# Performer attention and Fourier mixing on one core: head pairs on 128 partitions, alternating PE halves, rows turned through DRAM, 512-row channel blocks, a listed PE order

## The chip, the cores and the metric

The kernel runs on one core of one Trainium2 chip. The metric is the device time of one execution in microseconds; a median over several executions is given. A ratio "to before" is the mean time of one kernel's fast runs over the mean of the old kernel's fast runs of the same rounds on the same chip, so it is not quite the ratio of the medians.

Engine names are those of the profile: PE multiplies matrices, PEld is its weight load, DVE, ACT and POOL are the elementwise engines, SP issues transfers.

Two figures of mine recur. *Work* is the number of PE instructions of each kind, each at the spacing of starts that it has when nothing is waited for at full clock. *Lost* time is a stretch of the trace less the work whose starts fall in it. It covers both waiting and half-clock running.

## The reference, cut to what matters

```python
# q, k, v: (8, 8, 576, 64) float32; omega: (128, 64)
def phi(x):                                   # random features, 128 of them
    h = einsum('bhsd,md->bhsm', x, omega) - sum(x*x)/2
    return exp(h - max(h)) / sqrt(128)
q_p, k_p = phi(q*scale), phi(k*scale)
kv  = einsum('bhsm,bhsd->bhmd', k_p, v);  z = sum(k_p, axis=2)
att = einsum('bhsm,bhmd->bhsd', q_p, kv) / (q_p . z + 1e-6)
x   = att as (8, 576, 512)
u   = x + real(fft(fft(x, axis=1), axis=2))   # row and channel Fourier mix
un  = (u - mean(u)) / sqrt(var(u) + 1e-6)     # over the 512 channels
out = u + relu(un @ w_ch1) @ w_ch2            # 512 -> 2048 -> 512, weights float64
```

## The kernel before

Attention takes each head's 576 rows as 6 groups of 96 partitions (97 for the queries, whose rows are already put in the order that the folded Fourier transform wants). All six matmuls of one head's half of the array come one after the other:

```python
for i in range(2):                            # the two heads of a pair
    rows = slice(D * i, D * i + D)            # 64 of the 128 array rows
    kp = big_tile("kp")
    for r in range(R):                        # R = 6
        nc.tensor.matmul(kp[0:PR, ...], lhsT=kT[rows, r, :], rhs=omT[rows, :])
    kes.append(features(kp, PR, "ke"))
    # ... the same for qp, then kvp and ndp per head
```

Attention's result stays in SBUF, the mix works on it there, and the channel part takes the two halves of a batch, 289 rows each, as the moving operand; its second product comes out transposed and is turned back:

```python
for fc in range(NFC):                         # 16
    for dc in range(NDC):                     # 4
        nc.tensor.matmul(hp[:, 0:NK], lhsT=w1[...], rhs=un_t[:, dc, :], ...)   # NK = 289
    # ReLU to ht, on DVE for odd fc, on ACT for even
for dc in range(NDC):
    for fc in range(NFC):
        nc.tensor.matmul(op_[:, 0:NK], lhsT=w2[...], rhs=hs[fc][:], ...)
    # copy to SBUF, 128x128 transposes (otp), add, store
```

The float64 weights are narrowed to float32 on the chip, in 64 pieces of 256 columns, each with seven DVE instructions and one POOL addition. [cut: loads, tables, mix]

## Time and profile before

| | before |
|---|---|
| median | 1755.1 us (1749.4 to 1755.7) |
| PE busy | 1648 us, 94% of the span |
| PE work at full rate | 1523 us |
| lost before 400 us | 155 us |
| lost after 400 us | 71 us |

PE is busy all the time, but a busy PE is not a PE at its full rate. The prediction works from single starts; its 1528 us of work is the same sum from rounder prices.

### The profile page before, as it was taken

To read this page: it belongs to the slowest core of one execution; us is meant where nothing else is said; L and a number is where in the kernel's file an instruction comes from. 1 tells how busy PE (TensorE), PEld (TensorE's weight loads), DVE (VectorE), ACT (ScalarE), POOL (GpSimd) and SP (SyncE) were. 2 spreads that over 40 slices of the span, in tenths; PEclk is the share of its full clock that TensorE was granted. 3 is DMA by queue.
4 is the path that set the end of the run, shared out by engine and by line. 5 is a ranking of instruction groups with operands and counts; after the bars stand their busy time and mean duration, and the time that the engine had idled before them with its cause. 6 is when DMAs were issued, how large, how long until landed. Compare 5 with 4: busy or idle time off the path is not lost.

```text
span 1748.5 us, 21376 instructions
## 1 busy us (share of the span) xinstructions
PE 1648.2 (94%) x8897; PEld 1341.4 (77%) x8897; DVE 664.4 (38%) x1554; ACT 343.7 (20%) x609; POOL 233.2 (13%) x327
## 2 busy tenths in 40 slices
PE   6976888999999999999999999999999999998998
PEld 6864666877888788886888778887888778886776
DVE  5778776324233332414333332324233242333010
ACT  2211112112222221312122121212122121211000
POOL 2237332021000300021000300012000210012000
PEclk9995887999999999999999999999999999999999
DMA  6332222001010001101011010101011010000000
GB/s 136 80 81 68 72 87 77 21 8 27 22 41 21 16 19 28 41 8 28 21 35 27 1 35 21 48 8 28 21 30 26 7 28 22 20 1 14 0 14 14
DMA packets 125012, 56.92 MB, mean 33 GB/s; under 512 B 115762, under 2 KB 116018, under 8 KB 124916
## 3 DMA queue, kind: packets, MB, share of 16 engines
q1 hardware_dynamic: 119248, 37.83, 9.2%
q0 software_dynamic: 5120, 16.78, 3.1%
q8 instruction: 71, 1.16, 0.3%
q10 hardware_dynamic: 548, 0.94, 0.2%
q14 instruction: 25, 0.20, 0.0%
HBM read 46.09 MB, written 9.44 MB: 32 GB/s over the span
## 4 chain that ended last, share of the span: by engine, by line
PE 82%; DVE 8%; POOL 4%; DMA 3%; issue 1%; ACT 1%; POOLq 0%; DVEq 0%; ACTq 0%
PE hp L451 27%; PE op L470 25%; PE kvp L278 5%; PE qp L263 5%; PE kp L254 5%; PE ndp L304 4%; DMA raw<-in_moe_w_ch_dram 3%; PE yp L352 3%; PE eps L289 2%; DVE st L403 2%; POOL x L399 2%; PE tps L203 1%; PE otp L486 1%; PE fp L436 1%; PE tp L422 1%
## 5 line engine op out<-in xcount | busy, mean ns | idle before, releaser
L470 PE MATMUL op<-ht,w 128*128 128x289 f32 x2048 | 530.4, 413 | 7.1 <-POOL w L179 7.1
L451 PE MATMUL hp<-unT,w 128*128 128x289 f32 x2048 | 528.0, 411 | 1.8 <-DVE ht L460 1.7
L470 PEld LDWEIGHTS op<-ht,w 128*128 128x128 f32 x2048 | 384.6, 192 | 113.2 <-POOL w L179 8.2
L451 PEld LDWEIGHTS hp<-unT,w 128*128 128x128 f32 x2048 | 382.7, 191 | 113.7 <-issue 6.4
L460 DVE TENSOR_SCALAR ht<-hp 128x289 f32<-128x289 f32 x128 | 58.8, 459 | 372.2 <-PE hp L451 372.2
L122 POOL MEMSET v<- 96x12 f32 x32 | 3.8, 118 | 867.1 <-PE kvp L278 858.9
L254 PEld LDWEIGHTS kp<-omT,kT 64*96 64x96 f32 x768 | 98.4, 180 | 24.4 <-issue 16.6
L254 PE MATMUL kp<-omT,kT 64*96 64x128 f32 x768 | 113.9, 301 | 2.9 <-DVE qT L247 1.6
L263 PE MATMUL qp<-omT,qT 64*97 64x128 f32 x768 | 109.8, 296 | 6.9 <-DVE rstd L406 4.0
L462 ACT ACTIVATE ht<-hp 128x289 f32<-128x289 f32 x128 | 52.9, 413 | 291.6 <-PE hp L451 291.6
L278 PEld LDWEIGHTS kvp<-v,ke 96*128 96x128 f32 x768 | 103.4, 209 | 6.8 <-issue 1.1
L263 PEld LDWEIGHTS qp<-omT,qT 64*97 64x97 f32 x768 | 100.2, 181 | 10.8 <-ACT qT L241 5.1
L278 PE MATMUL kvp<-v,ke 96*128 96x65 f32 x768 | 105.3, 291 | 0.0
L221 ACT ACTIVATE ke<-ke 96x768 f32<-96x768 f32 x64 | 53.9, 842 | 215.3 <-DVE ke L215 215.3
L389 DVE SCALAR_TENSOR_TENSOR bmp<-ab,bmp 97x65 f32<-97x65 f32 x96 | 25.7, 328 | 175.2 <-ACT bmp L385 175.2
L304 PEld LDWEIGHTS ndp<-kv,qeT 128*97 128x97 f32 x768 | 82.2, 180 | 9.5 <-ACT qeT L295 1.6
L213 DVE TENSOR_REDUCE kemx<-kp 96x6 f32<-96x768 f32 x64 | 60.8, 950 | 71.4 <-PE kp L254 71.4
L492 DVE TENSOR_TENSOR x<-x,otp 97x512 f32<-97x512 f32 x48 | 32.3, 679 | 138.4 <-PE otp L486 138.4
L304 PE MATMUL ndp<-kv,qeT 128*97 128x65 f32 x768 | 82.7, 262 | 0.5 <-DVE kv L286 0.4
L480 ACT ACTIVATE ot<-op 128x289 f32<-128x289 f32 x64 | 26.5, 413 | 283.1 <-PE op L470 283.1
L295 ACT ACTIVATE qeT<-eps 128x582 f32<-128x582 f32 x64 | 42.0, 657 | 195.7 <-PE eps L289 180.6
L179 POOL TENSOR_TENSOR w<-ta,rest 128x256 f32<-128x256 f32 x64 | 53.8, 840 | 171.1 <-DVE rest L176 171.1
(73 smaller groups left out, 1413.5 us busy)
## 6 DMA issues: line engine op xcount, KB each, us to landing
raw<-in_moe_w_ch_dram POOLq DMA_DIRECT2D x64, 256.0 KB, 3.1
kn<-in_k_dram SPq DMA_DIRECT2D x64, 144.0 KB
qn<-in_q_dram SPq DMA_DIRECT2D x64, 144.0 KB
v<-in_v_dram SPq DMA_DIRECT2D x64, 144.0 KB
out_dram<-x SPq DMA_DIRECT2D x40, 192.0 KB
out_dram<-x SPq DMA_DIRECT2D x8, 190.0 KB
cs_sb<-k_cs ACTq DMA_DIRECT2D x1, 325.1 KB
sn_sb<-k_sn ACTq DMA_DIRECT2D x1, 325.1 KB
```

The lines of the kernel that those rows point to most:

```text
L179: nc.gpsimd.tensor_tensor(out=dst, in0=ta[:].bitcast(F32), in1=rest[:], op=ALU.add)
L213: nc.vector.tensor_reduce(mx[:], pr4, axis=AX.X, op=ALU.max)
L221: nc.scalar.activation(out=e[:], in_=e[:], func=AF.Exp, scale=SCALE)
L254: nc.tensor.matmul(kp[0:PR, r // 3, r % 3 * MF : r % 3 * MF + MF], lhsT=kT[rows, r, :], rhs=omT[rows, :],)
L263: nc.tensor.matmul(qp[0:CP, r // 3, r % 3 * MF : r % 3 * MF + MF], lhsT=qT[rows, t0 : t0 + CP], rhs=omT[rows, :],)
L278: nc.tensor.matmul(kvp[:, 0 : D + 1], lhsT=kes[i][:, r, :], rhs=v1[:, i, r, :], start=(r == 0), stop=(r == R - 1),)
L304: nc.tensor.matmul(nd[:, r, :], lhsT=qeT[:, r, :], rhs=kv[:])
L352: nc.tensor.matmul(yp[:, 0:NK], lhsT=fold[:, c, n, :], rhs=tab[:, c, :], start=(c == 0), stop=(c == NC3 - 1),)
L451: nc.tensor.matmul(hp[:, 0:NK], lhsT=w1[:, dc, 128 * fc : 128 * fc + 128], rhs=un_t[:, dc, :], start=(dc == 0), stop=(dc == NDC - 1),)
L460: nc.vector.tensor_scalar(ht[:], hp[:, 0:NK], 0.0, None, op0=ALU.max)
L462: nc.scalar.activation(out=ht[:], in_=hp[:, 0:NK], func=AF.Relu)
L470: nc.tensor.matmul(op_[:, 0:NK], lhsT=w2[:, fc, 128 * dc : 128 * dc + 128], rhs=hs[fc][:], start=(fc == 0), stop=(fc == NFC - 1),)
```

## The change

Its intent: PE does less, and the start overlaps better. Two heads of a pair share 128 partitions; their matmuls alternate between the upper and lower half of the array (or the left and right), so that two can run side by side. Attention's rows go to DRAM in plain order; the mix (the Fourier part) fetches the second half of the rows turned (in reversed order) by a gather, a transfer by a list of row numbers; the *fold* then adds and subtracts the two halves, first into the tile `half`, before the Fourier products `yp`; the mix's result goes through DRAM again, and the channel part takes blocks of 512 rows regardless of batches. The second product makes rows directly. PE's instructions follow a list that a small generator scheduler writes; other engines are ordered as before.

The core of the diff:

```diff
-            for i in range(2):
-                rows = slice(D * i, D * i + D)
-                kp = big_tile("kp")
-                for r in range(R):
-                    nc.tensor.matmul(kp[...], lhsT=kT[rows, r, :], rhs=omT[rows, :])
+            for j in range(3):
+                for par in range(2):
+                    rows = slice(D * par, D * par + D)
+                    nc.tensor.matmul(ps[:, par, MF * j : MF * j + MF],
+                        lhsT=kqT[rows, 3 * t + j, :], rhs=omT[rows, :])
 [cut: kvp alternates row halves, ndp column halves in the same way]
+        for c in range(NC3):
+            nc.gpsimd.indirect_dma_start(
+                out=x[:, NC3 + c, :], out_offset=None, in_=rows[:, :],      # 97 partitions
+                in_offset=bass.IndirectOffsetOnAxis(ap=turned[:, c : c + 1], axis=0))
+        yield 0.0, 5.0
 [cut: fold; first half of the sum on DVE, the difference on POOL, as before]
-                    nc.tensor.matmul(hp[:, 0:NK], lhsT=w1[...], rhs=un_t[:, dc, :], ...)
+                    nc.tensor.matmul(hp[:], lhsT=w1[...], rhs=unT[:, dc, :], ...)   # 512 rows
-                    nc.tensor.matmul(op_[:, 0:NK], lhsT=w2[...], rhs=hs[fc][:], ...)
+                    nc.tensor.matmul(yp[:], lhsT=hs[fc][:, 128*i : 128*i+128], rhs=w2[:, fc, :], ...)
-        ta = cvt.tile([128, n], U32, name="ta", tag="ta")
+        ta = cvt.tile([128, n], U32, name="ta", tag="ta", bufs=1)      # also tb and rest
+    with tc.manual_schedule(engines={mybir.EngineType.PE}):
+        streams = [weights(), mixing(), pairs(0), pairs(1), channels()]
 [cut: each stream's "yield work, latency" is the list's estimate in us; the first stream
  that is ready goes next]
```

## The prediction

> **What bounds the kernel now.** I read the page first (busy shares and the chain of work that ended last), then the table by stretches of time, then the timeline, because a busy PE is not yet a PE at its peak.
>
> ```profile
> PE 1648.2 (94%) x8897; PEld 1341.4 (77%) x8897; DVE 664.4 (38%) x1554; ACT 343.7 (20%) x609; POOL 233.2 (13%) x327
> ...
> PE 82%; DVE 8%; POOL 4%; DMA 3%; issue 1%; ACT 1%; POOLq 0%; DVEq 0%; ACTq 0%
> ```
>
> PE is busy for 94% of the span and carries 82% of the chain. So the kernel is bound by TensorE; other engines matter where they make it wait. Where that is, the table by stretches tells (columns: stretch, length, then busy time of PE, weight loads, DVE, ACT and POOL, granted clock, DMA share, GB/s):
>
> ```profile
> 0.00:127.00 127.00, 98.73 (x481) 92.17 (x481) 86.98 (x242) 27.41 (x37) 35.05 (x60) 1.00 0.42 100
> 127.00:185.00 58.00, 38.35 (x133) 28.07 (x134) 50.99 (x133) 9.65 (x19) 38.06 (x46) 0.59 0.23 65
> 185.00:312.00 127.00, 112.35 (x558) 88.14 (x557) 84.75 (x250) 22.65 (x37) 36.12 (x58) 0.87 0.26 77
> ...
> 312.00:1612.00 1300.00, 1268.20 (x7192) 1032.46 (x7191) 430.41 (x909) 273.29 (x491) 123.92 (x164) 1.00 0.09 23
> 1612.00:1748.00 136.00, 130.54 (x538) 100.58 (x537) 11.31 (x22) 10.72 (x26) 0.00 (x0) 0.98 0.03 9
> ```
>
> Until 312 us PE issues 1172 matmuls, against 7192 in the next 1300 us: 3.8 per us and then 5.5. In the start DVE works 223 of 312 us, mostly on narrowing the weights, and PE waits for it. What a matmul costs when nothing is waited for is in the timeline (start, length, engine, line, shapes, count), from one group's start to the next group's:
>
> ```profile
> 12.08 2.87 PE L254 MATMUL kp<-omT,kT 64*96 64x128 f32 x12
> ...
> 643.39 1.16 PE L304 MATMUL ndp<-kv,qeT 128*97 128x65 f32 x12
> 644.39 1.50 PE L278 MATMUL kvp<-v,ke 96*128 96x65 f32 x12
> 645.73 0.67 PE L289 MATMUL eps<-ident,qe 97*128 97x97 f32 x6
> 646.24 4.10 PE L451 MATMUL hp<-unT,w 128*128 128x289 f32 x16
> ...
> 664.06 1.55 PE L254 MATMUL kp<-omT,kT 64*96 64x128 f32 x12
> 665.45 1.47 PE L263 MATMUL qp<-omT,qT 64*97 64x128 f32 x12
> 666.85 4.16 PE L470 MATMUL op<-ht,w 128*128 128x289 f32 x16
> ```
>
> Per instruction: ndp 1.00/12 = 83 ns, kvp 1.34/12 = 112, eps 0.51/6 = 85, features (kp, qp) 2.79/24 = 116, against busy means of 262 to 301 ns in the table by lines, which count the pipeline's depth too. In the chain of waits the last 128 op matmuls take 31.15 us, 243.4 ns each: 289 columns at 1.2 per ns are 240.8, plus 2.6. A written f32 matmul is two instructions (384 kp matmuls in the code, 768 in the trace); a transpose is one.
>
> Priced so, PE's work in the old kernel is: channel mixing 4096 x 243.4 ns = 997 us. Attention per head pair: features 48 x 116, kvp 24 x 112, ndp 24 x 83, 24 transposes x 84 = 5.57 + 2.69 + 1.99 + 2.02 = 12.3 us, for 32 pairs 393. Fourier part 192 yp x 243 + 192 ab x 109 + 144 ab x 86 ns = 80. Transposes for the normalised rows 192 x 84 ns = 16, of the output 192 x 109 ns = 21, the flips (fp) 48 x 0.43 us = 21. In all 1528 us, so about 220 us of the span is not work at full rate. Counted with the same prices, about 158 us of the work falls before 311 us, so 153 of the 220 are lost in the start, the other 67 to waits later.
>
> **What the Trainium skill says.** (1) "TensorE: Matmul & The Clock Gate", Part 1: a PE with idle gaps is held at half its clock. The trace agrees: twelve kp take 2.87 us at 12.08 and 1.55 at 664.06. The clock column's 1.00 for the first stretch is then only a stretch without a record. (2) The same page, Part 3 (packing small matmuls): with 64 rows or columns in use, instructions on other row or column groups run side by side[...]. No group in this trace alternates its half, so the trace can't confirm it; the change rests on this. (3) "TensorEngine Tiling (Array Packing)", Key Properties: changing the tiling mode drains the array. The trace has something like it: single starts show 334 ns from an hp to a kp that follows, in place of 243, and 199 from a qp to an hp in place of 109, so 0.09 us a switch. (4) "DMA: Bandwidth & Descriptors", Specifications: transfers under 512 B do not reach line rate. The old kernel's loads are already so (115,762 of 125,012 packets), with DMA engines 9% busy later on; the new row stores in 256 B pieces should be borne likewise.
>
> **The change part by part.**
> Channel mixing in nine blocks of 512 rows instead of sixteen of 289: 9 x 128 = 1152 written matmuls, 2304 instructions. By the slope above, 512/1.2 + 2.6 = 429 ns; the new list's own 3.45 us for eight is 431. 2304 x 431 ns = 993 us: saves only 4. The pad rows were few and the fixed part is small.
> The second product now writes rows, not columns: the 192 output transposes go (-21). Rows are turned by an indirect transfer: the flips go (-21).
> Row transposes for the norm: 36 tiles x 4 = 144 of 128 columns, x 109 ns = 16: no change. Fourier part: same matmuls, 80.
> Attention per pair: 18 transposes of 128 x 109 ns = 2.0 us; 36 feature instructions, 36 kvp, 36 ndp. Without overlap of the halves: 36 x 109 + 36 x 112 + 36 x 56 (64 columns and 65 moving, 65/1.2 + 2.6) = 9.9, total 11.9 against 12.3: the fuller partitions alone buy next to nothing, since time goes by columns and the counts hardly fall. With overlap the features and kvp halve: 2.0 + 2.3 (the list's own figure for kvp), ndp 1.4 (list), total 7.7 us. Over 32 pairs 246 us, -147. Against it more mode switches: four stretches a pair (two of features, kvp, ndp), eight switches x 0.09 x 32 = 23 us.
> Work: 993 + 246 + 80 + 16 = 1335, with the switches 1358 us.
>
> **The start.** The chain is attention of batch 0, stores and reads through DRAM, mix, stores, reads, norm, first block. The order of w1 by output columns lets the first block start before all of it is there. But DVE is loaded: each narrow is 2.6 us of DVE (166 us over 64), each pair 6 x 0.95 + 0.3 + 0.5 + 0.9 = 7.4. With twelve pairs (88), two mixes (18), a norm and evictions (14) that is some 285 us by the point where the last w2 piece is there, and ta, tb and rest have one buffer now, so a narrow also waits for POOL's 0.84 us of the narrow before. I put the dense part's begin at about 310 us, with about 190 us of work done: 120 us lost, against 153.
> **Later waits.** Two pair streams take steps one after the other and share two large PSUM buffers. A feature tile is freed only after reduce and subtract (1.9 us), so the second stream's feature step waits about 3 us for the first's: 14 x 3 = 42. Last division to first yp: 1.3 us of DVE, two DRAM trips of estimated 2.5 and 5, fold 4.1, that is 13 to 16 us where the list allows 11; about 3 us a batch, 21 in seven. After that, a long stretch of nothing but blocks and row transposes, dense. The end: one addition and one store, 6 us.
> Sum: 1358 + 120 + 42 + 21 + 6 = 1547. The list was made to fill such waits with 3.45 us pieces of channel work, and some of what I add singly falls together, so I take 20 off: 1527 us.
>
> **Rivals.**
> A: the halves do not run side by side (the f32 passes, or the shared PSUM, serialise them). Then attention costs 11.9 us a pair and the time is 1527 + 32 x 4.2 = 1660. For it: nothing in this trace shows overlap. Against it: the code separates the halves into banks or partitions, and its stated 2.3 us for 36 kvp (64 ns) and 1.4 us for 36 ndp (39 ns) are below any serial price.
> B: the fixed PE order turns latencies into stalls: DRAM round trips, the fold on POOL (3.45 + 1.81 + 2 x 1.0 us), PSUM waits. If each batch loses 15 us more, and each pair 1.5, it is 1527 + 105 + 42 = 1674. For it: a late arrival holds all later PE work. Against it: after the list's PACE gaps only about half the kernel holds attention; the rest is channel work with no such wait.
> C: the start is much better than I think, channel work from 200 us on with w2 arriving in time: 60 us lost, 1467. For it: the old kernel started its channel work at 185 us already. Against it: its DVE was the limit then, and the amount of narrowing is unchanged.
> D: the reordered rows make DMA the bound. Estimated bytes grow from 57 to about 105 MB, 70 GB/s over the span; the first stretch already moves 100. I give it little.
>
> **Range and chances.** C below and A or half of B above give 1430 to 1620 us for 8 in 10. Even A with the waits as they are stays over 2% below 1755. Slower would take A and B together. Predicted 1527 us; faster 0.95, within 2% 0.03, slower 0.02.
>
> **What would show it.** Features, kvp and ndp of the new kernel: starts 55 to 64 ns apart in alternating groups (39 for ndp) if the overlap is real, 109 to 112 if A holds. Channel matmuls 429 to 433 ns apart. The first channel matmul at 150 to 200 us, and dense PE from about 310. Idle of PE before feature groups by DVE if the PSUM waits are real; before yp by DVE or DMA for B. PE's total falling by some 170 us of work, with losses of about 190 us beside it: if the work falls so and the time does not, the list made the waits and my sizes of them are wrong.

## The result, and the profile after

The changed kernel takes 1614.5 us (median of 4 runs, 1613.9 to 1616.3), the old one 1752.6 in its runs so far; the ratio is 0.921 (0.919 to 0.924). That is 8% faster. It lies inside the predicted range of 1430 to 1620, by 6 us, and 87 us above the predicted 1527.

The page's busy shares and the chain that ended last, of the changed kernel:

```profile
PE 1430.2 (89%) x7009; PEld 810.2 (50%) x7009; DVE 562.8 (35%) x1269; ACT 243.2 (15%) x389; POOL 304.3 (19%) x387
...
PE 68%; DMA 10%; DVE 7%; POOL 5%; issue 4%; ACT 0%; SPq 0%; POOLq 0%; DVEq 0%; ACTq 0%
```

PE has 218 us less to do by busy time, but its share of the chain fell from 82 to 68% and transfers came up from 3 to 10%. The kernel became shorter and waits more. The timeline of the changed kernel in a stretch at full clock (start, length, engine, line, shapes, count):

```profile
612.58 1.61 PE L272 MATMUL pp<-omT,kqT 64*128 64x128 f32 x24
614.12 3.70 PE L537 MATMUL op<-w,ht 128*128 128x512 f32 x8
...
619.22 0.94 PE L272 MATMUL pp<-omT,kqT 64*128 64x128 f32 x12
620.08 3.70 PE L537 MATMUL op<-w,ht 128*128 128x512 f32 x8
623.62 1.63 PE L394 MATMUL yp<-sn_sb,fold 97*128 97x289 f32 x6
625.18 2.23 PE L299 MATMUL kvp<-v,e 64*128 64x65 f32 x36
627.34 0.68 PE L409 MATMUL ab<-cd_sb,y 128*97 128x129 f32 x4
```

From one group's start to the next: features 1.54/24 = 64 ns and 0.86/12 = 72, kvp 2.16/36 = 60; ndp, at 601.87 in the same view, takes 1.20/36 = 33. In the old kernel these were 116, 107 to 112 and 83. Single starts within such a group lie about 7 ns apart and then a long gap: the two halves start nearly together. The prices include the switches at a group's ends. The slope of the prediction holds too: 243.4 ns for 289 columns and 109 for 128 (prediction) are 1.2 columns per ns, which gave 429 for 512, and 429 was measured. So the pieces of PE's work come out thus:

| | predicted | measured |
|---|---|---|
| channel matmuls, 2304 | 993 us (431 ns) | 989 us (429 ns) |
| attention, 32 pairs, with switches | 246 + 23 | 247 |
| Fourier part, row transposes | 96 | 95 |
| **work** | **1358** | **1331** |
| lost in the start (measured: before 400 us) | 120 | 200 |
| later waits (42 + 21, less 20) | 43 | 77 |
| end | 6 | 4 |
| **span** | **1527** | **1612** |

The work fell by 192 us. The waits did not shrink by 57 us as predicted; they grew by 55, from 226 to 281. The question for the experiments is where. The table by stretches, of the kernel before and then of the changed one (columns as in the prediction):

```profile
400.00:1200.00 800.00, 783.79 (x4464) 638.82 (x4463) 265.92 (x560) 170.80 (x304) 73.69 (x100) 1.00 0.10 24
1200.00:1748.00 548.00, 528.36 (x2807) 424.31 (x2805) 151.20 (x320) 99.27 (x184) 39.30 (x52) 0.99 0.07 18
```

```profile
400.00:1200.00 800.00, 753.17 (x4003) 420.34 (x4002) 237.49 (x473) 135.96 (x217) 131.78 (x146) 0.97 0.21 59
1200.00:1612.00 412.00, 408.39 (x1029) 186.94 (x1028) 48.52 (x100) 24.90 (x44) 18.35 (x29) 1.00 0.10 29
```

Once attention and mix are done (after 1200 us) the new kernel is dense: PE busy 408 of 412 us. Between 400 and 1200 it idles 47 us where the old one idled 16, and the clock is 0.97. Most of the idle comes in five pieces of 4.6 to 8.7 us, one for each mix after 400 us. One of them, on DVE and on PE:

```profile
1030.38 0.69 DVE L521 TENSOR_SCALAR ht<-hp 128x512 f32<-128x512 f32 x1 [6.17 <-PE hp L512]
...
1044.56 1.76 DVE L371 TENSOR_TENSOR half<-x 97x1536 f32<-97x1536 f32 x1 [13.49 <-DMA x<-xs,turned]
1046.36 0.96 DVE L372 TENSOR_TENSOR half<-half 97x765 f32<-97x765 f32 x1
1047.42 1.03 DVE L380 TENSOR_TENSOR fold<-half 97x384 f32<-97x384 f32 x2
1048.36 0.16 DVE L387 COPY mid<-half 97x3 f32<-97x3 f32 x1
1048.43 0.69 DVE L521 TENSOR_SCALAR ht<-hp 128x512 f32<-128x512 f32 x1
...
1049.17 17.12 PE L512 MATMUL hp<-unT,w 128*128 128x512 f32 x34 [8.53 <-DVE ht L521]
```

The brackets give the idle time before an instruction and what ended it. DVE stands still for 13.5 us because the fold's first addition (half) waits for the gather. The ReLU (ht) of a finished hp is behind it in DVE's order and comes only at 1048.43, so PE, whose two hp buffers are both full, stands for 8.5 us. Had one only read PE's line, the ReLU would have been blamed. The records show half clock for 10 us from 1044 us; as the stall lasts to 1049.2, PE's work meets the second half of it, and its first matmuls start 0.85 us apart in place of 0.43. Such stretches of 10 us stand also at 504, 849 and 1190 us, one of 7 us at 668: one for each of these five mixes.

The gather itself is out of proportion. In the profile's list of transfers of the changed kernel (times are issue to landing, last column):

```profile
x<-xs,turned POOLq DMA_INDIRECT x24, 12.2
us<-x,turned POOLq DMA_INDIRECT x24, 2.8
```

Both move rows of 2 KB by a list of row numbers. The first, 97 rows, takes 12.2 us, the second, 96 rows, 2.8. The Trainium skill has a rule that fits: "DMA: Bandwidth & Descriptors", section "Why a DMA increments its semaphore by 16 and not by 1", says of the number of DMA engines used that the generator takes the largest k up to 16 that divides the slowest dimension of both sides. 96 gives 16; 97 is prime and gives 1. The same section names an exception for some direct copies issued from POOL and does not speak of gathers, so it had to be tried. The share of all 16 engines during the three gathers of the mix at 1026 us (40 slices of 0.5 us, in tenths):

```profile
DMA  7000918999600044211432111112111100000000
```

From about 8 us on, apart from one short peak, only some 0.1 to 0.2 of 16 engines work, which is what three gathers on one engine each come to (3/16 = 0.19). Narrower windows of the same view are sharper: from 1037.5 to 1039 us, with three gathers under way, POOL's queue is busy for 19.5% of 16 engines, that is 3.1; from 1042 to 1043.5, with one left, for 6.6%, that is 1.06. So the packets of one gather follow each other one at a time. There is a second difference: POOL's queue has 25,856 packets in this kernel and 8,192 in the one with 96 rows below, the others nearly all of 8 bytes or less. They are done in the short peaks; the long tail is rows of data.

### The profile page after: what moved, and what is told of

Its sections match the earlier page's. It is cut to its first block, busy times and chain, and to the rows that moved or that the text cites. A ratio compares the mean times of both kernels' runs of the same rounds, so it can differ in the third digit from the quotient of the medians.

```text
span 1612.1 us, 17293 instructions
## 1 busy us (share of the span) xinstructions
PE 1430.2 (89%) x7009; PEld 810.2 (50%) x7009; DVE 562.8 (35%) x1269; ACT 243.2 (15%) x389; POOL 304.3 (19%) x387
## 3 DMA queue, kind: packets, MB, share of 16 engines
q0 software_dynamic: 25856, 26.41, 5.7%
## 4 chain that ended last, share of the span: by engine, by line
PE 68%; DMA 10%; DVE 7%; POOL 5%; issue 4%; ACT 0%; SPq 0%; POOLq 0%; DVEq 0%; ACTq 0%
PE op L537 29%; PE hp L512 23%; DMA x<-xs,turned 4%; PE kvp L299 3%; PE yp L394 3%; PE tps L242 3%; PE pp L272 3%; POOL x L356 2%; DMA raw<-in_moe_w_ch_dram 2%; DMA us<-x 2%; DMA us<-x,turned 2%; PE ndp L317 1%; PE ab L409 1%; POOL w L197 1%; PE tp L489 1%
## 5 line engine op out<-in xcount | busy, mean ns | idle before, releaser
L512 PE MATMUL hp<-unT,w 128*128 128x512 f32 x1152 | 521.2, 606 | 18.1 <-DVE ht L521 17.6
L537 PE MATMUL op<-w,ht 128*128 128x512 f32 x1152 | 513.0, 596 | 0.0
L512 PEld LDWEIGHTS hp<-unT,w 128*128 128x128 f32 x1152 | 218.1, 194 | 272.9 <-issue 248.0
L537 PEld LDWEIGHTS op<-w,ht 128*128 128x128 f32 x1152 | 213.3, 190 | 241.5 <-issue 235.9
L272 PE MATMUL pp<-omT,kqT 64*128 64x128 f32 x1152 | 95.6, 311 | 33.6 <-DVE e L281 25.5
L279 DVE TENSOR_REDUCE mx<-pp 128x6 f32<-128x768 f32 x96 | 91.3, 951 | 65.7 <-PE pp L272 65.7
L272 PEld LDWEIGHTS pp<-omT,kqT 64*128 64x128 f32 x1152 | 81.1, 212 | 64.6 <-issue 51.8
L299 PE MATMUL kvp<-v,e 64*128 64x65 f32 x1152 | 89.2, 319 | 11.5 <-DVE e L281 5.5
L299 PEld LDWEIGHTS kvp<-v,e 64*128 64x128 f32 x1152 | 85.1, 232 | 27.2 <-issue 26.8
L281 DVE TENSOR_TENSOR e<-pp,mx 128x768 f32<-128x768 f32 x96 | 91.6, 954 | 4.4 <-DVE mx L279 0.5
L394 PE MATMUL yp<-cs_sb,fold 97*128 97x289 f32 x96 | 31.9, 475 | 45.2 <-DVE fold L380 45.2
L317 PE MATMUL ndp<-kv,qeT 128*64 128x65 f32 x1152 | 43.3, 233 | 21.4 <-DVE e L281 12.4
```

The lines of the kernel that those rows point to most:

```text
L272: nc.tensor.matmul(ps[:, par, MF * j : MF * j + MF], lhsT=kqT[rows, 3 * t + j, :], rhs=omT[rows, :],)
L279: nc.vector.tensor_reduce(mx[:], pr4, axis=AX.X, op=ALU.max)
L281: nc.vector.tensor_tensor(out=e[:].rearrange("p (c two) m -> p two c m", two=2), in0=pr4, in1=mx[:].unsqueeze(3).to_broadcast([P, 2, 3, MF ...
L299: nc.tensor.matmul(kvp[:, i, 0 : D + 1], lhsT=feature(r)[rows], rhs=v1[rows, r, :], start=(r == 0), stop=(r == R - 1),)
L317: nc.tensor.matmul(ndp[cols, r // 5, (D + 1) * (r % 5) : (D + 1) * (r % 5 + 1)], lhsT=qeT[:, r, cols], rhs=kv[:, i, :],)
L394: nc.tensor.matmul(yp[:, 0:NK], lhsT=fold[:, c, n, :], rhs=tab[:, c, :], start=(c == 0), stop=(c == NC3 - 1),)
```

## The experiments

Twelve kernels ran, all correct but the two that were made wrong. Every ratio is to the old kernel.

### The gather's row count

```diff
-                out=x[:, NC3 + c, :], ...
-                in_offset=...(ap=turned[:, c : c + 1], axis=0),
+                out=x[0:CW, NC3 + c, :], ...                       # CW = 96
+                in_offset=...(ap=turned[0:CW, c : c + 1], axis=0),
+        for c in range(NC3):
+            s0 = S - CW * (c + 1)
+            nc.sync.dma_start(x[CW:CP, NC3 + c, :], rows[s0 : s0 + 1, :])
```

> Edit: each gather of turned rows takes 96 rows in place of 97; the 97th row comes by a plain 2 KB copy. Theory L (the long gather): the 97-row gathers land in 12.2 us, the 96-row scatters of the same row size in 2.8 us, and the fold's first addition waits for them at the head of DVE's in-order queue, so PE waits for evictions queued behind it. Then the gather should land in about 3 us, idle of DVE before the half addition fall from 80 us to under 20, and the time fall by 50 to 100 us (seven or eight batches at 7 to 11 us, plus the half-rate clock that follows each stall), to 1515-1565 us. Rival P (the gather is slow because of POOL's descriptor work or HBM, not because of the row count): landing stays above 8 us and the time moves less than 20 us.

Measured: 1547.5 us, ratio 0.884 (0.881 to 0.888), 67 us less than the changed kernel. Landing fell to 4.9 us (median), POOL's time to issue one from 2.17 to 0.93 us:

```profile
x<-xs,turned POOLq DMA_INDIRECT x24, 4.9
```

In the late mix at 1116 us the share of DMA engines in the 20 us from 1118 us reads

```profile
DMA  9999995000000000000000000000000000000000
```

all sixteen busy, done in under 4 us (the first two digits are mostly the plain load of the first half; from 1119.5 to 1121 us the gathers' queue alone takes 96.8% of 16 engines). DVE's idle before the half addition fell from 80 to 20 us, just at the limit I had set. Lost time after 400 us fell from 81 to 28 us, and half clock after 400 us from 48 to 2 us. In the start only 15 us were gained. One row in 97, moved separately, is worth 4% of the kernel.

### Is it the gather, or its place in DVE's order?

First try: allow more time in the list, so that the fold comes later.

```diff
-        yield 0.0, 5.0      # after the mix's loads
+        yield 0.0, 20.0
```

> Edit: the list's allowance after the mix's loads goes from 5 to 20 us; the gathers stay as they are (12.2 us). Theory L: it is the place of the fold's addition in DVE's order that makes the long gather cost anything; with it some 15 us later, the PE stalls for ReLU evictions at the mixes go although the gather is as slow as before, and the part after 400 us shortens by 40 to 70 us; the start may lengthen by up to 15 us since batch 0's chain is stretched. Total 1555-1590 us. Rival: the mixes themselves bound the end (their data is late for the channel blocks); then stretching them makes the kernel slower, above 1620 us.

Measured: 1593.5 us, ratio 0.908 (0.907 to 0.910): 21 us faster, less than expected, and not a test of the theory. The list orders PE alone; in DVE's order the half additions after 400 us stand within two places of where they stood, and they still waited 45 us for the gather there. Where the 21 us come from was not followed up. The second try takes the waiting addition off DVE:

```diff
-            ((nc.vector, ALU.add, ALU.add), (nc.gpsimd, ALU.subtract, ALU.subtract))
+            ((nc.gpsimd, ALU.add, ALU.add), (nc.gpsimd, ALU.subtract, ALU.subtract))
 [and the allowances after loads and fold go from 5 and 6 to 16 and 8 us]
```

> Edit: the 97-row gather stays (about 12 us to landing), but the fold's sum half moves from DVE to POOL, so that no DVE instruction waits for the gather; the list's allowances for loads and fold go to 16 and 8 us to cover it. Theory H (head of the line: DVE's order, not the gather as such, costs PE time): PE's waits for ReLU evictions and for the feature subtraction after 400 us fall from 40 us to under 10, and the time falls by 30 to 60 us, to 1555-1585 us. Rival (the gather is slow for everyone, PE would wait for the fold itself instead): waits before yp take their place and the time stays within 20 us of 1614.

Measured: 1560.4 us, ratio 0.891 (0.889 to 0.894): 54 us faster, with the gather as slow as ever (12.3 us). PE's waits after 400 us, as the list of waits has them:

```profile
PE pp L272 <- DVE xo L331: 2.0, 3, 0.7
PE tp L489 <- DVE u L483: 1.9, 1, 1.9
PE pp L272 <- DVE e L281: 1.5, 1, 1.5
PE tps L242 <- issue: 1.5, 2, 0.8
PE hp L512 <- DVE ht L521: 1.4, 1, 1.4
```

In the changed kernel the same list begins

```profile
PE hp L512 <- DVE ht L521: 16.6, 2, 8.5
PE ndp L317 <- DVE e L281: 10.6, 3, 8.7
```

and goes on with 7.7 us for kv: DVE instructions that, in their longest waits, stood behind half. Lost time after 400 us fell from 81 to 30 us, half clock there from 48 to 2 us, while the start lost as much as before (198 us). So theory H holds: with no instruction that PE needs soon behind its reader, a transfer of 12 us cost PE next to nothing after 400 us. Nor was the fold itself needed soon: in the changed kernel the first yp of a mix after 400 us starts 64 to 126 us after the mix's half addition on DVE (1122.0 against 1044.6 us in the mix shown), so the addition stood that much too early in DVE's order. The edit also stretched the list, as the first try did, and its share of the 54 us is not separated; the first try's 21 us is the nearest figure for it, not a bound.

### Do the halves make the gain?

```diff
-                for j in range(3):
-                    for par in range(2):
+                for par in range(2):
+                    for j in range(3):      # kvp and ndp: all r of one half, then the other
```

> Edit: same matmuls, but all of one row or column half before all of the other, in features, kvp and ndp. Theory O (the gain is the side-by-side halves): starts go from 64-72, 60 and 33 ns apart to about 110-116, 107-112 and 56-62; per pair +1.9 +1.8 +0.9 = 4.6 us, for 32 pairs about +145 us, less what falls into waits in the start (8 to 12 pairs run there, at half clock): +100 to +150, 1715-1765 us, so the change's whole gain would be gone. Rival (the gain is from channel blocks, fewer transposes, layout): below +60 us.

Measured: 1735.3 us, ratio 0.988 (0.984 to 0.991): 121 us slower, nearly all of the change's gain. The timeline of this run:

```profile
729.37 1.26 PE L272 MATMUL pp<-omT,kqT 64*128 64x128 f32 x12
730.57 3.70 PE L537 MATMUL op<-w,ht 128*128 128x512 f32 x8
734.20 3.84 PE L299 MATMUL kvp<-v,e 64*128 64x65 f32 x36
737.96 3.70 PE L512 MATMUL hp<-unT,w 128*128 128x512 f32 x8
```

kvp is at 3.76/36 = 104 ns, features at 1.20/12 = 100 (1.86/24 = 77 in groups of 24), ndp at 57. Per pair that is 0.65 + 1.6 + 0.9 = 3.1 us more, 100 us in all. The 145 expected were too many mostly for the features: in the group of 24 at 723.88 us nine starts follow the one before by 4 to 6 ns, though the list changes the half only three times, so the run on one half begins before the run on the other has ended. The other 20 us, by difference, are added waits. The counterpart is the old kernel with this one part of the change, for its feature matmuls alone:

```diff
+            kpp = [big_tile("kp") for i in range(2)]
+            for r in range(R):
+                for i in range(2):           # the two heads alternate
+                    rows = slice(D * i, D * i + D)
+                    nc.tensor.matmul(kpp[i][...], lhsT=kT[rows, r, :], rhs=omT[rows, :])
 [the same for qp]
```

> Edit: the kernel before, with one part of the change alone: the feature matmuls of the two heads of a pair alternate between row halves. 48 of them a pair go from 116 to about 65 ns: 2.4 us a pair, 78 us over 32 pairs; less what lies in the start: 45 to 78 us faster than 1754, 1676-1709 us. Rival (halves do not pay without the new layout, since two feature tiles must be held in PSUM at once): under 25 us.

Measured: 1707.0 us, ratio 0.974 (0.972 to 0.976): 45 us faster, at the edge of the expectation. qp is at 62 ns in three groups of four (83 in the others); for kp every second group is at 62, the others at 113 to 153 with starts 109 ns apart: there the halves do not run side by side. Why is not shown: a wait for the second tile's buffer would be a guess, since PE's list of waits after 400 us has none. Counted at 62 and 113 ns, work falls by some 65 us, and 20 of them come back as lost time. The halves pay without the new layout, but not in full.

### What does the start lose?

In the changed kernel 200 us are lost before 400 us, in the old one 155. Its narrowing ends at 356 us, not at 296. PE's longest wait in the start is for the fold, here and with the 96-row gather:

```profile
PE yp L394 <- DVE fold L380: 45.2, 3, 24.7
PE yp L397 <- DVE fold L383: 26.1, 3, 12.5
```

In the old kernel, whose mix works in SBUF, PE's waits for the fold in its first 312 us come to 12.3 us. Is DVE's narrowing behind it?

```diff
 [in narrow: seven DVE instructions replaced by one, result wrong on purpose]
+        nc.vector.tensor_scalar(ta[:], hi, 0x3CFFFFFF, None, op0=ALU.bitwise_and)
+        nc.gpsimd.tensor_tensor(out=dst, in0=ta[:].bitcast(F32), in1=ta[:].bitcast(F32), op=ALU.add)
```

> Edit: the seven DVE operations that narrow a piece of weights become one (result wrong on purpose); the loads and POOL's addition stay. DVE loses about 140 us of work, all in the first 400 us. Theory N (DVE's narrowing bounds the start): the 200 us lost before 400 us (time less matmuls at full rate) fall by 60 to 110 us, total 1505-1555 us. Rival (the start is set by the chain attention-DRAM-mix-DRAM-norm and by half clock, or by the weights' loads on POOL's queue): less than 30 us.

Measured: 1588.9 us, ratio 0.907 (0.904 to 0.910): 26 us gained, inside the rival's limit of 30. Since the gather's stalls are still in this kernel and may hide part of it, the same edit ran on top of the 96-row gather:

> Edit: the 96-row gather together with the one-operation narrow (wrong on purpose). If DVE's narrowing is what the start still loses, the 185 us lost before 400 us in the kernel with the 96-row gather fall by 40 us or more, 1490-1510 us; if the chain of loads, DRAM trips and half clock is, by less than 25, 1522-1545 us. From the cheap narrow alone (25 us gained) I expect some 25 to 35: 1512-1522.

Measured: 1512.5 us (ratio 0.863, 0.861 to 0.865), 35 us less than with the gather alone. Lost time before 400 us goes from 185 to 152, between the two limits set, all of it after 160 us; DVE's busy time there fell from 286 to 169 us. In the first 160 us 100 us are lost in every one of these kernels (the old one, the changed one, and these two with and without the 96-row gather), and the first row transpose comes at 159 to 168 us.

Then the buffers of the narrow (ta and rest back to two):

> Edit: the 96-row gather, and ta and rest of the narrow back to two buffers as in the kernel before. DVE waited 23 us in 30 pieces for POOL's addition of the piece before. If that holds the start back, 10 to 20 us less than 1547; if other DVE work fills those waits or the path is elsewhere, within 6 us of it.

Measured: 1547.5 us, ratio 0.883 (0.881 to 0.885), no change at all. The waits for POOL's addition fall from 18.7 to 3.9 us (before 400 us), but those for the loads of the next weights grow from 24 to 46 us; the last piece is narrowed at 331 us, 15 us earlier than with the 96-row gather alone, and PE gains nothing by it: its waits for the fold after 160 us stay at 24 us.

Half the clock is granted for 183 us of the run with the 96-row gather, nearly all in the start. Is it a cause? PE was kept busy with products that nobody reads:

```diff
+    def warm():
+        while there["w2"] < NFC:
+            wp = mmp.tile([128, TB], F32, name="wp", tag="mm")
+            nc.tensor.matmul(wp[:], lhsT=ident[:], rhs=wz[:])
+            yield 0.87, 0.0
```

> Edit: the 96-row gather, and in the start, where the list finds no stream ready, PE multiplies the identity by a constant tile (results unread, correct output) until the last weights are there. In the first 160 us PE does about 60 us of full-rate work and loses 100 us in every variant so far, most of it with matmuls at half rate. Theory C (the half clock itself holds the start back): the feature and kvp groups of the first 160 us run at full rate for longer, and the loss before 400 us falls by 20 us or more, 1505-1527 us. Rival (latencies of DVE, loads and DRAM trips hold it back; a warm PE only waits longer): the dummies add their own time, 1545-1580 us.

Measured: 1565.7 us, ratio 0.894 (0.891 to 0.896): 18 us slower. It did warm PE: kvp of the first two pairs took 4.24 us where it had taken 7.94, and half clock fell from 183 to 109 us. Yet the first row transpose came later (175 us), and lost time in the first 160 us stayed at 101 (the products themselves count as lost). So taking much of the half clock away gained nothing here. It is not a clean test, since the products take PE's time (150 of them ran) and one of the two PSUM buffers of the channel matmuls.

Two edits of the list's spacing, pairs first:

```diff
-                yield 0.0, PACE
+                yield 0.0, (PACE if there["w2"] == NFC else 50.0)
```

> Edit: the 96-row gather, and pairs of later batches spaced by 50 us in place of 25 until the last weights are in the list. Fewer pairs share DVE with the narrowing in the start (some 4 fewer, 30 us of DVE). If early pairs crowd out the weights, 10 to 20 us less than 1547; if the delayed pairs are then missed by the blocks later (a batch is wanted every 110 us or so), it gives that back: within 10 us of 1547 or slower.

Measured: 1559.4 us, ratio 0.890 (0.888 to 0.892), 12 us slower. The start gained 9 us (177 lost of the first 400), and the 600 us after it lost 23 us more, as the rival said. Then the weights, one piece per 3.0 us of the list's time:

```diff
-                    yield 0.0, 3.0
+                    yield 0.0, 4.5          # and 2.0 in the other run
```

> Edit: the 96-row gather, and the list takes a piece of weights every 4.5 us of its own time in place of 3.0, so that batch 0's chain shares DVE with fewer pieces. If the order of DVE's work in the start can be improved this way: first channel matmul 10 us or more earlier than 183 us, total 1525-1540 us. If DVE's amount of work bounds the start whatever its order: first channel matmul earlier but the second product later, within 10 us of 1547 or slower.

> Edit: the opposite, a piece every 2.0 us. Weights done earlier than 345 us, first channel matmul later than 183 us. Under a bound by the amount of DVE work the two shift cancel, within 10 us of 1547; if the weights' arrival is what holds the second product (first op at 308 us), 1525-1540 us.

Measured: 1568.8 us (ratio 0.896, 0.894 to 0.899) with 4.5, and 1532.8 us (0.875, 0.874 to 0.877) with 2.0. The last piece is narrowed at 359 us, 345 us (3.0) and 322 us; the time follows by +21 and -15 us. With 4.5 the first channel matmul hardly came earlier (181 us, not 183), so that order gained nothing. With 2.0 it is later (192 us), and so is the first of the second product (325 us, not 308): the time is the one forecast, but not by the way forecast. The gain comes between 320 and 400 us, where the lost time falls from 27 to 3 us. There PE waits for the third mix's fold 12.5 us with 3.0 and 17.0 us with 4.5; with 2.0 this wait is 0.4 us, and its list has channel and attention work at that place. When the weights are there does not decide it alone: with two buffers they were there at 331 us, and the wait (12.4 us) and the time stayed. Which of the shifts in the list removes the wait was not tested. The run with 2.0 and the 96-row gather, 1532.8 us, is the fastest correct kernel of this study.

## Why the prediction was right or wrong

The range and the direction were right; the gain is 138 us of the 228 forecast. The range held by 6 us, and in part by luck: the start was 80 us worse than forecast and the later waits 34, while the work came out 27 us better.

*Work.* Right, and for the reason given. The overlap of the halves, which no line of the old trace could show, is there, and rival A is refuted by the starts 7 ns apart and by the serial run. Its own size of +133 us was closer to the measured 121 than my later expectation of the serial run. The eight switches a pair were counted twice: the measured 60, 33 and 64 to 72 ns hold them, so the 23 us were too much (246 without them was right). Channel blocks of 512 rows saved 8 us of work, 4 forecast.

*The start.* This is the largest miss: "I put the dense part's begin at about 310 us, with about 190 us of work done: 120 us lost, against 153". The dense part begins at about 400 us and 200 us are lost. The prediction had DVE's load of 285 us in the start, and then let it run nearly without gaps; the trace has DVE busy for 277 of 400 us. Narrowing ends at 356 us. And DVE's load is not what sets the begin: with 117 us of it taken out (169 in place of 286 us) the start still loses 152 us, more than the 120 forecast for the full load. What the sum left out is the chain through DRAM, which the prediction names but does not price in the start: PE stands 45.2 us for the folds of the first three mixes. The runs name two parts: the long gather (15 us, 96-row gather) and DVE's narrowing (33 us, cheap narrow on top). The buffers that I blamed are worth nothing (run with two buffers). What the first 160 us lose, 100 us in these variants, is not explained by narrowing, and the filled start did not lower it; the old kernel loses as much there. That stays open.

*Later waits.* The step failed in its terms more than in its sum. "14 x 3 = 42" for PSUM waits of the second pair stream: in the run with the 96-row gather all PE waits after 400 us, those for PSUM among them, come to under 8 us. In the changed kernel PE's feature matmuls do wait for the subtraction 15 times, 25.5 us in all, but every time before 400 us. "About 3 us a batch, 21 in seven" for the trip through DRAM had the right place and the wrong mechanism: it took the loads at an estimated 5 us, when the gather needs 12.2, and it had PE waiting for the fold. In the start PE did wait for the fold; after 400 us it never did. There it waited for ReLUs and features behind the fold in DVE's order, and found half clock after it. The 96-row gather takes 53 us off the lost time after 400 us. Rival B ("a late arrival holds all later PE work") described it best, though it named PE's fixed order, where DVE's order did the harm.

*The 20 us taken off for overlap of these terms* had no ground in any view.

*Rivals C and D.* C is refuted: channel work did begin at 187 us, but the second product only at 314. D is refuted for bandwidth: DMA engines were busy for about 23% of the time (the shares of all queues); each slow gather had one engine's worth of them (1.06 of 16).

With the gather mended the kernel takes 1547.5 us, 20 us above the prediction. In its trace the start is 65 us worse than forecast (185 against 120), the work 27 us less and the other waits 21 us less (28 against 49).

## What to carry to other kernels

Before moving rows by a list or a stride, look at the number of partitions: one row too many cost 67 us here. (96 and 97 are all that was tried; that a multiple of 16 is the safe choice is the DMA page's rule.) When an engine with fixed order reads a late transfer, ask not only who needs its result, and when (here 64 to 126 us later), but what stands behind it in that engine's order; moving the reader to another engine gained nearly as much as mending the transfer. When a new layout is priced, check whether the count of instructions or their columns fall at all: here fuller partitions gave almost nothing, and letting two halves of the array run side by side gave nearly everything.

## What the Trainium skill lacked or had wrong

- "DMA: Bandwidth & Descriptors": it gives the rule for the number of engines, but no time for a gather by row numbers, and its exception for some direct copies issued from POOL leaves open whether a gather is spread; the runs fit the rule, not the exception. 97 rows of 2 KB land in 12.2 us, 96 in 4.9 us (3.3 in a late mix); POOL's own issue takes 2.17 and 0.93 us, and a 97-row gather brings some 736 more packets, nearly all of 8 bytes or less.
- "TensorE: Matmul & The Clock Gate", Part 3, and "TensorEngine Tiling (Array Packing)": neither has a figure for f32 with two halves of 64. Here features run at 64 to 72 ns an instruction against 116 in the old kernel, kvp at 60 against 104 when serial, ndp with column halves at 33 against 57, starts of a pair 7 ns apart; the figures include the switches at a group's ends.
- The same clock page, Part 1 and its list of aims, would have a kernel keep PE busy to hold the full clock. Filling the start with unread products did cut half clock, from 183 to 109 us, as the page has it, and made the kernel 18 us slower: the page has no case in which the work that keeps PE busy is useless.
- No page has a word on the order that a compiler's scheduler gives the other engines when only PE is listed: in the run with an allowance of 20 us in place of 5 the waiting DVE instruction stayed within two places of where it was, and the gain was 21 us where taking it off DVE gave 54.
